# Three key tiles in a burst of value matmuls instead of two, in the sequence part of an attention and Fourier kernel

## The chip, the core and the metric

The kernel runs on one core of a Trainium2 chip. The metric is device time in microseconds (us) of one execution; each kernel is run several times and the median counts. The core's engines work side by side and wait for each other by semaphores: TensorE (PE; its weight loads are shown apart as PEld), VectorE (DVE), ScalarE (ACT), GpSimd (POOL), and SyncE (SP), which here only issues DMAs. Matmul results land in PSUM, which has eight banks of 512 fp32 columns on 128 partitions. Everything else lies in SBUF.

## The reference

The result is a gate between an attention block and a two-dimensional Fourier transform of the same x (2048 rows, 640 columns, 32 heads of 20):

```python
def _A_ref(x, wqkv, wo):
    qkv = (x @ wqkv).reshape(B, S, 3, H, Dh)  # to q, k, v by head
    scores = jnp.einsum("bhqd,bhkd->bhqk", q, k) * (Dh ** -0.5)
    p = _softmax(scores, axis=-1)
    o = jnp.einsum("bhqk,bhkd->bhqd", p, v)
    return o.reshape(B, S, D) @ wo
def _B_ref(x, dft_seq_re, dft_seq_im, dft_hid_re, dft_hid_im):
    a = jnp.einsum("bsd,ed->bse", x, dft_hid_re)
    b = jnp.einsum("bsd,ed->bse", x, dft_hid_im)
    return jnp.einsum("ts,bse->bte", dft_seq_re, a) - jnp.einsum("ts,bse->bte", dft_seq_im, b)
g = _sigmoid((x * gate_w).sum(-1, keepdims=True))
return g * _A_ref(x, wqkv, wo) + (1 - g) * _B_ref(x, ...)
```

Products that need fp32 precision are made of three matmuls on rounded parts: a number is split into a rounded first part and the rest (`split`, L110), and `part1*part1 + part1*rest + rest*part1` is summed.

## The kernel before

After an opening stage (projections to q, k, v, up to about 250 us), the kernel is one long stream of attention work with other matmuls poured into its gaps.

**Attention.** 32 units follow each other; a unit is a pair of heads and half of the queries. A unit has 32 *steps*; a step is one key tile of 128 keys by 512 queries, for both heads. For each step PE does two score matmuls, called `e`: one for each head, keys by queries (L907). ACT takes their exponent out of PSUM into an SBUF tile `p` (L909). The softmax needs the largest score of each query beforehand. For that PE computes the scores a second time, queries by keys, 41 steps ahead; these two score matmuls a step are called `m` (L187), and DVE reduces each of them to its row maxima (L189). When a unit's maxima are complete, they are reduced once more (L203), transposed on PE (L221), split (L114, L115) and sent by four small DMAs into spare rows of the query stack (L229, L230). The two heads sit in partitions 0 to 63 and 64 to 127, so a score matmul uses one half of PE's rows and two of them can run side by side.

**Value matmuls.** Two steps make one key tile for all 1024 queries of the unit. For each key tile PE does four matmuls of the exponents with the values (L528), for two heads and two query blocks, each in its own quarter of PE's columns. They add up in one PSUM bank, `av`, over the 16 key tiles of a unit. At a unit's end ACT copies `av` out (L536). These are fp32 matmuls, and the trace shows each as two records.

**Cycles and fills.** The stream is cut into cycles of four steps. A cycle is written out as a string: `e`, `m`, `F` (a fill) and `B`. `B` is the burst, the value matmuls of two key tiles in a row. An `F` is one or two fill units. A fill unit is two matmuls of 320 columns, one in each half of the rows, into the banks `yp0` and `yp1`. There are three parts of the stream by what the fills are: the hidden transform (56 cycles, L363), the sequence transform (168 cycles, L608, from about 608 to 1668 us), and the output projection (32 cycles, L715).

**PSUM.** Scores take turns in five banks, `ps0` to `ps4` (`bank`): a score matmul must wait until ACT or DVE has read the score five places earlier. `av`, `yp0` and `yp1` are the other three banks.

**The sequence part.** It consists of seven products of eight *blocks* each (56 blocks). A block is one output tile of 128 rows: 16 sequence tiles, three fill units each, so 48 fill units in three cycles. For the stationary side, a chunk of 1024 columns of the transform matrix, eight sequence tiles, is loaded by SP into a `raw` tile. POOL then adds a second matrix to it where the product asks for it (L501, products 0, 2, 3, 5 and 6 counted from 0) and splits it into a `part` tile (L114, L115). A block takes two chunks. There are three `part` buffers; each chunk's split is put on POOL's queue in the middle of the chunk two before it. For the moving side, 16 tiles `x` of the next product are made during the present one from its second block on: loaded into `araw`, added where asked for (L517), split (L114, L115). This is a *preparation*; `run_extras` does at most one in a burst. At a block's end ACT and DVE sum the two banks (L627, L628), and POOL adds the result to earlier partial results (`finish_y`, L742). POOL also does the final multiplication of each attention unit (L560).

POOL executes its queue strictly in the order written, as each engine does.

## Time and profile before

| | us |
|---|---|
| runs of before | 1867.67, 1870.73, 1872.45 (median 1870.73) |
| the profiled execution | 1869.47 |
| its span, first to last instruction | 1867.7 |
| PE, DVE, ACT, POOL busy | 1858.3, 1383.7, 1272.1, 1162.6 |

The profile has instructions with their start, duration and the event that ended the idle time before them. Records of PE matmuls overlap, so "busy" says that something was in flight, not that PE ran at its peak. The granted clock is 0.98 in the first 100 us, 0.97 in the last stretch, and 1.00 in every 100 us between; so durations can be compared across the stream.

### The profile page before, as it was taken

To read this page: it belongs to the slowest core of one execution; us is meant where nothing else is said; L and a number is where in the kernel's file an instruction comes from. 1 tells how busy PE (TensorE), PEld (TensorE's weight loads), DVE (VectorE), ACT (ScalarE), POOL (GpSimd) and SP (SyncE) were. 2 spreads that over 40 slices of the span, in tenths; PEclk is the share of its full clock that TensorE was granted. 3 is DMA by queue.
4 is the path that set the end of the run, shared out by engine and by line. 5 is a ranking of instruction groups with operands and counts; after the bars stand their busy time and mean duration, and the time that the engine had idled before them with its cause. 6 is when DMAs were issued, how large, how long until landed. Compare 5 with 4: busy or idle time off the path is not lost.

```text
span 1867.7 us, 45004 instructions
## 1 busy us (share of the span) xinstructions
PE 1858.3 (100%) x17606; PEld 1360.8 (73%) x17606; DVE 1383.7 (74%) x2310; ACT 1272.1 (68%) x2439; POOL 1162.6 (62%) x1038
## 2 busy tenths in 40 slices
PE   9999999999999999999999999999999999999998
PEld 8988777676767777777777777767777777776666
DVE  3044458787878888888888888888888888888853
ACT  4222258787877777777777777777777777778885
POOL 3335432121146897466799899867779989635544
PEclk9999999999999999999999999999999999999999
DMA  6744341222134674535567576546476766431233
GB/s 230 174 136 151 139 127 56 78 65 68 54 99 139 209 209 142 161 128 175 185 192 241 163 249 191 176 140 179 145 240 203 214 198 202 142 90 47 88 98 108
DMA packets 178771, 281.61 MB, mean 151 GB/s; under 512 B 44811, under 2 KB 113547, under 8 KB 178559
## 3 DMA queue, kind: packets, MB, share of 16 engines
q1 hardware_dynamic: 177599, 276.77, 47.4%
q0 software_dynamic: 960, 1.97, 0.6%
q8 instruction: 138, 2.26, 0.5%
q14 instruction: 74, 0.61, 0.1%
HBM read 214.61 MB, written 63.52 MB: 149 GB/s over the span
## 4 chain that ended last, share of the span: by engine, by line
PE 98%; DMA 1%; POOL 0%; ACT 0%; DVE 0%; issue 0%; SPq 0%; POOLq 0%; ACTq 0%
PE av L528 25%; PE yp L608 19%; PE ps L907 16%; PE ps L187 15%; PE yp L363 7%; PE ps L118 4%; PE ps L120 4%; PE ps L119 4%; PE yp L715 3%; PE ps L221 0%; DMA p<-in_xa 0%; POOL p L115 0%; DMA a_scr<-raw 0%; DVE mx L189 0%; ACT p L323 0%
## 5 line engine op out<-in xcount | busy, mean ns | idle before, releaser
L189 DVE TENSOR_REDUCE mx<-ps 128x1 f32<-128x512 f32 x2048 | 1280.1, 684 | 298.9 <-PE ps L187 280.7
L909 ACT ACTIVATE p<-ps 128x512 f32<-128x512 f32 x2048 | 1109.1, 599 | 371.6 <-PE ps L187 248.9
L187 PE MATMUL ps<-kst,qst 60*128 60x512 f32 x1920 | 758.3, 410 | 0.0
L907 PE MATMUL ps<-qst,kst 62*128 62x512 f32 x1920 | 744.9, 407 | 0.1
L608 PE MATMUL yp<-x,part 64*128 64x320 f32 x5376 | 662.1, 306 | 0.3 <-ACT raw L373 0.3
L608 PEld LDWEIGHTS yp<-x,part 64*128 64x128 f32 x5376 | 624.7, 186 | 8.3 <-ACT raw L373 0.6
L528 PE MATMUL av<-p,v 128*21 128x512 f32 x4096 | 490.1, 596 | 0.0
L907 PEld LDWEIGHTS ps<-qst,kst 62*128 62x128 f32 x1920 | 348.1, 185 | 182.5 <-DVE mx L189 132.2
L187 PEld LDWEIGHTS ps<-kst,qst 60*128 60x128 f32 x1920 | 342.2, 184 | 7.9 <-issue 4.2
L115 POOL TENSOR_TENSOR part<-raw,part 128x1024 fp32r<-128x1024 f32 (+1 forms) x128 | 288.0, 2250 | 10.3
L528 PEld LDWEIGHTS av<-p,v 128*21 128x21 f32 x4096 | 97.6, 100 | 221.5 <-issue 218.3
L363 PE MATMUL yp<-wb,x 64*128 64x320 f32 x1920 | 224.0, 307 | 0.0
L374 POOL TENSOR_TENSOR raw<-raw 128x320 f32<-128x320 f32 x64 | 55.7, 870 | 268.4 <-ACT raw L373 219.1
L363 PEld LDWEIGHTS yp<-wb,x 64*128 64x128 f32 x1920 | 210.1, 186 | 6.0
L114 POOL CAST part<-raw 128x1024 fp32r<-128x1024 f32 (+1 forms) x128 | 126.1, 985 | 127.9 <-PE ps L187 67.0
L501 POOL TENSOR_TENSOR raw<-raw,raw 128x1024 f32<-128x1024 f32 x77 | 185.9, 2414 | 7.5 <-DMA raw<-in_cdft 6.0
L115 POOL TENSOR_TENSOR x<-araw,x 128x320 fp32r<-128x320 f32 x112 | 97.8, 873 | 9.0
L715 PE MATMUL yp<-x,part 64*128 64x320 f32 x768 | 102.2, 308 | 0.0
L323 ACT ACTIVATE p<-ps 128x512 f32<-128x512 f32 x40 | 23.8, 597 | 102.0 <-PE ps L120 85.5
L715 PEld LDWEIGHTS yp<-x,part 64*128 64x128 f32 x768 | 92.0, 186 | 1.0
L118 PE MATMUL ps<-x,part 128*128 128x512 f32 x200 | 80.7, 403 | 1.6 <-ACT x L112 1.3
L114 POOL CAST p<-p 128x512 fp32r<-128x512 f32 x40 | 24.7, 618 | 92.4 <-ACT p L323 92.4
(110 smaller groups left out, 1419.5 us busy)
## 6 DMA issues: line engine op xcount, KB each, us to landing
raw<-in_cdft SPq DMA_DIRECT2D x192, 512.0 KB
araw<-a_scr SPq DMA_DIRECT2D x192, 160.0 KB
qk_scr<-p SPq DMA_DIRECT2D x40, 512.0 KB
kst<-qk_scr SPq DMA_DIRECT2D x84, 160.0 KB
qst<-qk_scr SPq DMA_DIRECT2D x84, 160.0 KB
yt<-y_scr SPq DMA_DIRECT2D x80, 160.0 KB
a_scr<-raw SPq DMA_DIRECT2D x64, 160.0 KB
y_scr<-yt SPq DMA_DIRECT2D x64, 160.0 KB
```

The costliest lines, as they stand in the source:

```text
L114: e1.tensor_copy(dst1, src)
L115: e2.tensor_tensor(dst2, src, f32(dst1), op=ALU.subtract)
L118: pe.matmul(ps, st1, mv1, start=first, stop=False)
L187: pe.matmul(ps, q[b : b + KROWS, qt * P : (qt + 1) * P], k[b : b + KROWS, kc * 512 : (kc + 1) * 512], start=True, stop=True)
L189: return lambda: dve.tensor_reduce(mx[n][:, h, qt, kc : kc + 1], ps, axis=AX.X, op=ALU.max)
L363: pe.matmul(yp[h][:, :HE], x[r, xz, d, cs], w[r, wz, d, :HE], start=d == 0 and z == 0, stop=d == ND - 1 and z == 2)
L501: pool.tensor_tensor(raws[0], raws[0], raws[1], op=ALU.add if PRODUCTS[n][0][1][0] > 0 else ALU.subtract)
L528: pe.matmul(av[32 * j : 32 * j + DH + 1, :], v[:, kt, h * (DH + 1) : (h + 1) * (DH + 1)], pp[qc][:, h, :], start=kt == 0, stop=kt == NS - 1)
L608: pe.matmul(yp[h][:, :HE], c[r, cz, cs], a[r, az], start=s == 0 and z == 0, stop=s == NS - 1 and z == 2)
L715: pe.matmul(yp[h][:, :HE], o[oz][r], wos[d, hf][r, wz], start=d == 0 and z == 0, stop=end)
L907: pe.matmul(pt, k[b : b + KROWS + 2, kt * P : (kt + 1) * P], q[b : b + KROWS + 2, qc * 512 : (qc + 1) * 512], start=True, stop=True)
L909: act.activation(pts[n, kt, qc][:, h], pt, AF.Exp, scale=float(DH) ** -0.5)
```

## The change

A cycle of the sequence part now has six steps: twelve `e`, twelve `m`, 24 fill units, and a burst of three key tiles. A block has two such cycles. The other parts keep four steps and two key tiles. The strings and the places of the fills:

```diff
 ORDERS = (
     ("ememFFFeFFmeFFmFeFmFeFmFmFFeFemB", (0, 0, 1, 0), (1, 1, 0, 1)),
+    ("ememeFFFFmeFFemFeFmFemFeFeFmeFFmeFFFFmmemmB", (0, 0, 0, 1, 0, 1), (1, 1, 0, 1, 0, 0)),
+    ("emFeFmFeFFmFeFFmeFFmeFFmFmFeFmeB", (1, 0, 1, 1), (0, 1, 0, 0)),
     ("emFFeFmFeFFmFeFmFeFFmeFmFFmFemeB", (0, 1, 1, 0), (1, 0, 0, 1)),
-    ("emFeFmFeFFmFeFFmeFFmeFFmFmFeFmeB", (1, 0, 1, 1), (0, 1, 0, 0)),
 )
...
 for u in range(UNITS):
-    edge.append(edge[-1] + 3)
+    edge.append(edge[-1] + 2)
...
 def burst(c):
     for n in ends:
         max_nm(n)
-    run_extras(max(done - HIDS, 0) // 3, 2)
-    for kt in (2 * c, 2 * c + 1):
-        av_step(now[0], kt // NS, kt % NS)
+    k, _, i = phase(c)
+    steps = 6 if k == 1 else 4
+    run_extras(steps - 2)
+    run_preps()
+    for kt in range(i // 2, (i + steps) // 2):
+        av_step(now[0], kt // NS, kt % NS, kt % NS == 0 and kt > i // 2)
...
             else:
                 score(kind)
+            if k == 1 and x == len(order) // 2:
+                run_preps()
```

`run_preps` is the second half of the old `run_extras`; in the sequence part it is called in the middle of a cycle too, so four times a block, where it was three times.

Since 16 key tiles don't divide by three, a burst can hold the end of one unit and the start of the next. The `av` bank is then not a fixed one: six banks are in the ring, one of them is `av`, and a unit that starts inside a burst takes the bank that was used longest ago and gives the old one back. A new `av` has 32 columns of each head's values written (not 21), so that all of its 128 partitions are defined. The value tile gets 16 more columns, which POOL clears.

```diff
-    def bank():
-        return ps_w.tile([P, 512], F32, name=f"ps{next(turn) % 5}")
+    places = collections.deque(f"ps{k}" for k in range(6))
...
+    def next_av():
+        places.append(av["name"])
+        av["name"] = places.popleft()
+        av["tile"] = place_tile(av["name"])
```

Seven steps' exponents are alive at a burst, so `p` has seven buffers (it had five). The room comes from `part`: four buffers of 4 KB a partition, not three of 8 KB. A chunk is split in two halves of 512 columns (four sequence tiles), each into a buffer of its own, the first in the middle of the chunk two before it, the second at the start of the chunk before it. The addition is done once, ahead of the first half.

```diff
     def pair_tile():
-        return work.tile([P, 2, 512], F32, name="p", bufs=5)
+        return work.tile([P, 2, 512], F32, name="p", bufs=7)
     def part_tile():
-        return work.tile([P, 2, 1024], R, name="part", bufs=3)
+        return work.tile([P, 2, 512], R, name="part", bufs=4)
...
-        def finish():
-            c = cparts[g] = part_tile()
-            if len(raws) > 1:
+        def finish(half):
+            if not half and len(raws) > 1:
                 pool.tensor_tensor(raws[0], raws[0], raws[1], op=ALU.add if PRODUCTS[n][0][1][0] > 0 else ALU.subtract)
-            split(c[:, 0], c[:, 1], raws[0], pool, pool)
+            c = cparts[2 * g + half] = part_tile()
+            split(c[:, 0], c[:, 1], raws[0][:, half * 512 : (half + 1) * 512], pool, pool)
...
+        if s % 8 == 0 and g and cfin:
+            cfin.pop(0)()
         if s % 8 == 0 and g // 8 + 3 < 2 * UNITS:
-            cfin.append(load_c(g // 8 + 3))
-        if s % 8 == 4 and cfin and g // 8 + 2 < 2 * UNITS:
+            cfin.extend(load_c(g // 8 + 3))
+        if s % 8 == 4 and cfin:
             cfin.pop(0)()
...
-                extras.append((now[0] + 5, functools.partial(finish_y, out_, t, m, y)))
+                extras.append((now[0] + 3, functools.partial(finish_y, out_, t, m, y)))
```

What moves on PE, around one burst of the sequence part. Before, three scores, the burst (`av`, two key tiles of four matmuls), two scores, and then fills (`yp`):

```order
L907 MATMUL ps_18836<-qst_92,kst_90 128x512
L187 MATMUL ps_18839<-kst_89,qst_91 128x512
L907 MATMUL ps_18842<-qst_92,kst_90 128x512
L528 MATMUL av<-p,v 21x512 x8
L907 MATMUL ps_18864<-qst_92,kst_90 128x512
L187 MATMUL ps_18867<-kst_89,qst_91 128x512
L608 MATMUL yp_18870<-x_16422,part 128x320
```

In the changed kernel (L940 is the old L907, L196 the old L187, L546 the old L528, L628 the old L608), at a burst in which a unit ends after the first key tile:

```order
L196 MATMUL ps_14347<-kst_87,qst_89 128x512
L196 MATMUL ps_14350<-kst_87,qst_89 128x512
L940 MATMUL ps_14353<-qst_89,kst_87 128x512
L196 MATMUL ps_14356<-kst_87,qst_89 128x512
L196 MATMUL ps_14359<-kst_87,qst_89 128x512
L546 MATMUL ps_12559<-p,v 32x512 x4
L546 MATMUL ps_14379<-p,v 32x512 x8
L940 MATMUL ps_14390<-qst_89,kst_87 128x512
L196 MATMUL ps_14393<-kst_87,qst_89 128x512
L940 MATMUL ps_14396<-qst_89,kst_87 128x512
L196 MATMUL ps_14399<-kst_87,qst_89 128x512
L940 MATMUL ps_14406<-qst_89,kst_87 128x512
```

Five scores, four of them for maxima, now stand ahead of the burst, and five behind it before the first fill.

What moves on POOL, at the start of the preparations in product 3, where both the matrix and the `x` tiles have an addition. Before, three preparations stand among two chunks:

```order
L742 TENSOR_TENSOR yt<-yt,m 128x320 x2
L517 TENSOR_TENSOR araw<-araw 128x320
L114 CAST x_16422<-araw 128x320
L115 TENSOR_TENSOR x_16422<-araw,x_16422 128x320
L501 TENSOR_TENSOR raw<-raw,raw_16228 128x1024
L114 CAST part<-raw 128x1024
L115 TENSOR_TENSOR part<-raw,part 128x1024
L517 TENSOR_TENSOR araw<-araw 128x320
L114 CAST x_16422<-araw 128x320
L115 TENSOR_TENSOR x_16422<-araw,x_16422 128x320
L501 TENSOR_TENSOR raw<-raw,raw_16370 128x1024
```

In the changed kernel (L762 is the old L742, L532 the old L517, L515 the old L501, L115 and L116 the old L114 and L115) one preparation stands ahead of each half chunk:

```order
L762 TENSOR_TENSOR yt<-yt,m 128x320 x2
L532 TENSOR_TENSOR araw<-araw 128x320
L115 CAST x_16541<-araw 128x320
L116 TENSOR_TENSOR x_16541<-araw,x_16541 128x320
L115 CAST part<-raw 128x512
L116 TENSOR_TENSOR part<-raw,part 128x512
L532 TENSOR_TENSOR araw<-araw 128x320
L115 CAST x_16541<-araw 128x320
L116 TENSOR_TENSOR x_16541<-araw,x_16541 128x320
L515 TENSOR_TENSOR raw<-raw,raw_16411 128x1024
L115 CAST part<-raw 128x512
L116 TENSOR_TENSOR part<-raw,part 128x512
```

The 16 preparations of a product thus stand among the parts of four blocks, where they stood among those of more than five.

## The prediction

> **What bounds the kernel now.** I read the chain that ended last first (shares of the span by engine), then the sequence part as one window (length; busy us and instructions of PE, PEld, DVE, ACT, POOL; clock; DMA share), then the same window for the value matmuls alone:

> ```profile
> PE 98%; DMA 1%; POOL 0%; ACT 0%; DVE 0%; issue 0%; SPq 0%; POOLq 0%; ACTq 0%
> ```

> ```profile
> 607.80:1668.10 1060.30, 1060.30 (x10767) 762.24 (x10765) 889.52 (x1485) 766.82 (x1422) 851.63 (x682) 1.00 0.58 182
> ```

> ```profile
> 607.80:1668.10 1060.30, 321.62 (x2688) 63.90 (x2688) 1.00 0.58 182
> ```

> PE is never idle there: the end is set by PE's own stream, at full clock. The 2688 records are 168 bursts of 16. Whether "busy" is also useful is read from one cycle, in PE's timeline (start, duration, count) and, for the burst's inside, in PEld's:

> ```profile
> 1005.68 1.92 PE L528 MATMUL av<-p,v 128*21 128x512 f32 x16
> 1007.53 0.49 PE L907 MATMUL ps<-qst,kst 62*128 62x512 f32 x1
> 1007.53 0.49 PE L187 MATMUL ps<-kst,qst 60*128 60x512 f32 x1
> 1007.86 0.60 PE L608 MATMUL yp<-x,part 64*128 64x320 f32 x5
> ...
> 1011.62 0.40 PE L187 MATMUL ps<-kst,qst 60*128 60x512 f32 x1
> 1011.65 0.39 PE L907 MATMUL ps<-qst,kst 62*128 62x512 f32 x1
> 1011.97 1.92 PE L528 MATMUL av<-p,v 128*21 128x512 f32 x16
> ```

> ```profile
> 1006.13 0.12 PEld L528 LDWEIGHTS av<-p,v 128*21 128x21 f32 x4 [0.31 <-issue]
> 1006.55 0.12 PEld L528 LDWEIGHTS av<-p,v 128*21 128x21 f32 x4 [0.31 <-issue]
> ```

> A cycle lasts 6.29 us, burst to burst. From the first fill (1007.86) to the next burst (1011.97) are 4.11 us, of which the last 0.10 is the step into the burst. In the other 4.01 each half of the rows streams 7 scores of 512 columns and 16 fills of 320, 8704 columns: 0.461 ns a column, so a score takes 0.236 and a fill 0.147. All 8 scores and 16 fills of a half are 4.25 us. Four records abreast in the burst start 0.43 apart (1006.13 to 1006.55; the mean of the burst is 0.43), so four such rounds are 1.72. 6.29 - 4.25 - 1.72 leaves **0.32 us a cycle that is neither**: the scores after a burst last 0.49 instead of 0.39, the burst's last round takes longer until the next score starts, and there is the step into it.

> **What the change removes.** 168 bursts become 112 of one and a half times the work. 56 times 0.32 goes: **-17.9 us**. The new cycle would be 1.5 x (4.25 + 1.72) + 0.32 = 9.28 us. Value records, scores and fills stay as many; 32 columns of weights for 21 change only loads that lie beside matmuls (0.12 of each 0.43). The opening, the hidden part and the output part keep their order but for one cycle; I cost them at nothing, and so the 16-column clearing and the two added `p` buffers.

> **What it asks of DVE and ACT.** A score needs its bank read five scores later. DVE and ACT in that cycle (idle time before in brackets), and the sum of the two banks, once a block:

> ```profile
> 1008.09 5.07 DVE L189 TENSOR_REDUCE mx<-ps 128x1 f32<-128x512 f32 x8 [1.23 <-PE ps L187]
> ```

> ```profile
> 1008.16 3.34 ACT L909 ACTIVATE p<-ps 128x512 f32<-128x512 f32 x6
> ```

> ```profile
> 1019.62 0.49 DVE L628 TENSOR_TENSOR m<-yp,m 128x320 f32<-128x320 f32 x1 [0.17 <-ACT m L627]
> ```

> DVE reads one score in 0.63, so 12 of them take 7.6 of 9.28 us. In a burst PE gives it nothing for 6 x 0.43 + 0.32 = 2.9 us, but four of the last five scores are maxima, 2.5 us of work that lies under it. ACT's twelve take 6.7 us (0.56 each). Both fit, with little to spare: going through the new order place by place with 0.236 and 0.147, the tightest places (the `e` after one fill in the middle, and the `m` before the six fills) come when DVE is just done. The same tightness can be seen in the hidden part, whose cycle has 15 fills for 16 and also starts with four scores in a row:

> ```profile
> 445.62 1.91 PE L528 MATMUL av<-p,v 128*21 128x512 f32 x16
> 451.79 1.92 PE L528 MATMUL av<-p,v 128*21 128x512 f32 x16
> ```

> 6.17 us, where 6.29 less one fill is 6.14: 0.03 lost a cycle. I take this for the new cycle: 112 x 0.03 = **+3.4 us**, and a cycle of 9.31. The bounds are 0 and 0.2 a cycle, +22 us, if one place waits a third of a DVE reduction (0.2 of 0.63); no gain is to be had, since the sequence part now loses nothing there. DVE's sum at a block's end (0.49) stands behind the four maxima under the burst, and the transposition for a unit's maxima comes as often as now.

> **What it asks of POOL.** This is the dear part. POOL in product 3 (starts give what each really occupies), the half-size split as it occurs in the output part, and POOL's load by product (length, busy us; products 1, 2, 3, 5):

> ```profile
> 1103.92 1.29 POOL L560 TENSOR_TENSOR o<-o,rb 128x512 f32<-128x512 f32 x1
> 1105.17 2.41 POOL L501 TENSOR_TENSOR raw<-raw,raw 128x1024 f32<-128x1024 f32 x1
> ...
> 1111.12 0.88 POOL L517 TENSOR_TENSOR araw<-araw 128x320 f32<-128x320 f32 x1
> 1112.06 0.45 POOL L114 CAST x<-araw 128x320 fp32r<-128x320 f32 x1
> 1112.59 0.87 POOL L115 TENSOR_TENSOR x<-araw,x 128x320 fp32r<-128x320 f32 x1
> 1113.42 2.41 POOL L501 TENSOR_TENSOR raw<-raw,raw 128x1024 f32<-128x1024 f32 x1
> 1115.89 1.04 POOL L114 CAST part<-raw 128x1024 fp32r<-128x1024 f32 x1
> 1117.01 2.39 POOL L115 TENSOR_TENSOR part<-raw,part 128x1024 fp32r<-128x1024 f32 x1
> 1119.37 1.70 POOL L742 TENSOR_TENSOR yt<-yt,m 128x320 f32<-128x320 f32 x2
> 1121.02 0.88 POOL L517 TENSOR_TENSOR araw<-araw 128x320 f32<-128x320 f32 x1
> ...
> 1714.77 0.61 POOL L114 CAST part<-raw 128x512 fp32r<-128x512 f32 x1
> 1715.46 1.29 POOL L115 TENSOR_TENSOR part<-raw,part 128x512 fp32r<-128x512 f32 x1
> ```

> ```profile
> 759.30:911.00 151.70, 90.54 (x77) 1.00 0.48 149
> 911.00:1062.46 151.46, 138.16 (x108) 1.00 0.63 200
> 1062.46:1214.09 151.63, 138.78 (x114) 1.00 0.66 206
> ...
> 1365.49:1517.08 151.59, 139.46 (x109) 1.00 0.66 203
> ```

> A preparation is 2.30 (1111.12 to 1113.42), an addition 2.47, a chunk's split 3.48 (1115.89 to 1119.37), two `finish_y` 1.65, the final multiplication 1.25. A half split is 0.69 + 1.26 = 1.95 (the next one starts 0.03 before a subtraction's recorded end), so a chunk costs 3.90 for 3.48: **0.42 more, 112 times**. Alone that is free where POOL has room (60% busy in product 1). Products 2, 3 and 5 are 91 to 92% busy over their whole length, and more during the preparations, which now come two a cycle. One cycle uses one chunk: 2 x 2.30 + 2.47 + 3.90 = 10.97 us of POOL against 9.31 of PE. POOL falls behind by 1.66 a cycle, plus its other work.

> How much of that can it bear? In product 1 a chunk's split waits for PE to give back its buffer, and starts at once when the last fill on it has ended (cast and its wait; PE's last fill of that chunk):

> ```profile
> 839.37 1.04 POOL L114 CAST part<-raw 128x1024 fp32r<-128x1024 f32 x1 [3.67 <-PE ps L187]
> ```

> ```profile
> 838.99 0.45 PE L608 MATMUL yp<-x,part 64*128 64x320 f32 x3
> ```

> So I start from a POOL that waits for buffers. In the new order a cycle's first 12 fill units end about 3.6 us into it (13 scores and 12 fills by the prices above, and the 0.3 that a fill takes to land), and its first fill stands at 0.8. In cycle X the first half is given back at 3.6 and split at 5.55. Then come, in product 3, two `finish_y` (1.65), a preparation, a half, a preparation, an addition and a half (2.30 + 1.95 + 2.30 + 2.47 + 1.95): 18.2. That half is needed at 3 x 9.31 + 0.8 = 28.7, a margin of 10.5. The remaining seven prepared cycles cost POOL 7 x 10.97 + 3 x 1.65 + 1.25 = 83.0 and PE 65.2: the margin ends at -7.3, and PE waits that long in all. In products 2 and 5 (one `finish_y` a block): margin 11.3, then 80.5 against 65.2, **-4.0** each. In product 0 (none): 12.1, 78.0 against 65.2, -0.7. In products 1 and 4 the chunks have no addition, and there is room. Together 7.3 + 4.0 + 4.0 + 0.7 = **+16.0 us**. After the preparations POOL needs about 7 of 9.31 a cycle and catches up before the next product's. The bounds are 0 and 25: a microsecond of margin counts about 3.5 times, and I trust the margin to 2.5 us. Before, the same account gives 2 x 5.95 + 3 x 2.30 + 1.65 = 20.5 against 18.9 a block, under 1.6 behind for 5.3 blocks, which the margin covers; and indeed no wait for POOL shows on PE.

> [...]

> **The sum.** -17.9 + 3.4 + 16.0 = +1.5 us on the profiled execution's 1869.47 (span 1867.7 and 1.8 around it): 1871.0. That execution is 1.3 under the median of the three runs, 1870.73, so against the median it is 1872.3. I say **1872**: no change that shows. The two large terms are of one cause each and of opposite signs.

> **Rivals.**
> - *POOL's lag doesn't reach PE.* It needs 7.3 us more margin than I count in product 3. For it: POOL's spans are rough, and no wait of this kind is in the trace. Against: the casts' and subtractions' starts repeat to 0.1 us, and the load is a plain sum. Time: 1872.3 - 16.0 = 1856, 0.8% faster.
> - *The banks become the bound.* Four maxima at the end of a cycle and five scores before the first fill leave DVE always just in time; from a wait of 0.1 us a cycle on, the loss counts. At 0.2 a cycle: +22.4. The cycle is then 9.48, which gives POOL's margin 0.17 x 10 = 1.7 more in each product: 16.0 falls to about 10. -17.9 + 22.4 + 10 = +15, so 1885, slower. For it: DVE's 1.23 of idle time a cycle lies wholly in the burst now, and the burst grows by 0.86. Against: DVE's share of the cycle doesn't rise by more than 0.32 in 18.9. [...]
> - *The bursts' transition isn't saved whole*, because a change of bank inside a burst (two of three units) costs as much as a cycle's: 14 of the 21 unit ends there, 0.1 to 0.3 each, under 5 us. It shifts the sum within the forecast's own range.

> **How the numbers follow.** Forecast, within 5.6 us of 1870.73 (0.3%, about what a measurement here can tell from no change): 0.40. POOL's lag at most half of what I count, the first rival and the way to it: 0.34. Banks, or POOL worse than counted: 0.26. So faster 0.34, same 0.40, slower 0.26. The range goes from the first rival's 1856 to the second's 1885; its ends leave out a tenth on each side. The forecast's own range is 1865 to 1877.

> **What would show it.** In the changed profile: bursts of 24 records, 112 of them, 9.28 to 9.31 us apart in products 1 and 4 (6.29 and 0.32 right); longer cycles only in the later preparations of products 3, 2 and 5, with PE's or PEld's fills waiting for POOL's `part` subtraction, 7, 4 and 4 us in all; POOL without idle time there. Cycles of 9.4 or more everywhere, with scores waiting for DVE, would be the second rival; none longer than 9.31, the first. Late maxima rows (the four small DMAs now have four steps of time in one unit of three) would show as `e` scores that wait for a DMA; I expect none.

## The result, and the profile after

The changed kernel takes **1900.12 us** (median of four runs, 1899.02 to 1903.87) against 1869.40 for the kernel before on the same chip (four runs, 1867.67 to 1872.45). The ratio is 1.0166, with a 95% interval of 1.0145 to 1.0187: 31 us slower. The prediction said 1872 and, at the most, 1885. The profiled execution took 1903.9 us (span 1902.1).

The same three views as before, for the changed kernel: the chain that ended last, the sequence part as one window, and in it the value matmuls.

```profile
PE 87%; DMA 6%; POOL 5%; issue 1%; DVE 0%; ACT 0%; SPq 0%; POOLq 0%; DVEq 0%; ACTq 0%
```

```profile
609.66:1699.90 1090.24, 1071.71 (x10749) 776.57 (x10747) 885.26 (x1481) 715.88 (x1418) 884.15 (x914) 0.99 0.59 176
```

```profile
609.66:1699.90 1090.24, 315.05 (x2688) 76.53 (x2688) 0.99 0.59 176
```

The chain is PE for 87% of the span, where it was 98%; 11% are now transfers and POOL. PE is idle for 18.5 of the 1090 us (1090.24 less 1071.71), where it was never idle, and its mean clock is 0.99, not 1.00. The sequence part is 30 us longer. So the loss is waiting, and something with the clock.

Where PE waits, its own timeline says (start, duration, count; in brackets the wait and what ended it). Of nine waits over 0.3 us in the sequence part, these are five:

```profile
993.87 0.49 PE L196 MATMUL ps<-kst,qst 60*128 60x512 f32 x1 [2.92 <-DVE mx L198]
...
1167.08 0.41 PE L628 MATMUL yp<-x,part 64*128 64x320 f32 x2 [1.60 <-POOL part L115]
1168.44 0.56 PE L628 MATMUL yp<-x,part 64*128 64x320 f32 x4 [0.33 <-POOL part L116]
...
1203.96 0.79 PE L196 MATMUL ps<-kst,qst 60*128 60x512 f32 x1 [3.76 <-DVE mx L198]
...
1519.49 0.79 PE L196 MATMUL ps<-kst,qst 60*128 60x512 f32 x1 [5.72 <-DVE mx L198]
```

The other four are 1.65 and 0.88 for DVE, 0.77 and 0.33 for POOL. In all PE waits 14.9 us for DVE and 3.0 for POOL's parts. The wait that I predicted is there and smaller than forecast; the large one is another.

**What DVE waits for.** The longest case, in the timeline of the changed kernel: ACT's copy of a unit's output, what SP issues after it, DVE, and PE.

```profile
1489.05 0.60 ACT L554 ACTIVATE o<-ps 128x512 f32<-128x512 f32 x1 [1.49 <-PE ps L546]
...
1500.66 0.55 SPq L562 DMA_DIRECT2D l_scr<-o  x1
1501.26 0.96 SPq L881 DMA_DIRECT2D qst<-qk_scr  x2
1503.06 0.35 SPq L768 DMA_DIRECT2D y_scr<-yt  x1
1504.17 2.75 SPq L510 DMA_DIRECT2D raw<-in_cdft  x2
1506.96 1.03 SPq L881 DMA_DIRECT2D qst<-qk_scr  x2
1508.04 0.34 SPq L565 DMA_DIRECT2D lc<-l_scr  x1
...
1511.37 1.29 DVE L198 TENSOR_REDUCE mx<-ps 128x1 f32<-128x512 f32 x2 [0.18 <-PE ps L196]
1518.64 0.25 DVE L568 RECIPROCAL lc<-lc 128x16 f32<-128x16 f32 x1 [5.99 <-DMA lc<-l_scr]
...
1513.13 0.64 PE L628 MATMUL yp<-x,part 64*128 64x320 f32 x4
```

At a unit's end its softmax sums (one row for each head and query block in `o`) go out by a DMA (`store_l`, L562) and come back spread over 128 partitions (`load_l`, L565). DVE takes their reciprocal (L568). The reciprocal stands at a fixed place of DVE's queue, 16 steps behind the unit's end, and the maxima written behind it start only after it (the next at 1518.81). Here the sums were stored 11.0 us after `o` was complete (1489.65) and their load was issued 18.4 us after it. DVE is done with the maxima ahead of the reciprocal at 1512.66, and stands for 5.99 us. All maxima behind it wait; PE's scores find no free bank and PE stops at 1513.8. The same steps in the kernel before, for the same unit:

```profile
1462.17 0.60 ACT L536 ACTIVATE o<-av 128x512 f32<-128x512 f32 x1 [0.98 <-PE av L528]
...
1476.39 0.33 SPq L547 DMA_DIRECT2D lc<-l_scr  x1
...
1485.79 0.24 DVE L550 RECIPROCAL lc<-lc 128x16 f32<-128x16 f32 x1
```

There the load was issued 13.6 us after `o` and the reciprocal found it landed, at 23.0. Over all units of the sequence part the load came at the latest 15.4 us after `o` before the change; after it, six came between 19.0 and 22.9. SP's waits (total us, times, longest) show why SP, which issues nearly all DMAs (1456 of the 1468 in the trace), one after the other as they are written, is late. First before, then after:

```profile
SPq L512 <- POOL araw L517: 32.3, 15, 4.3
...
SPq L495 <- POOL raw L501: 31.4, 16, 5.9
```

```profile
SPq L527 <- POOL araw L532: 68.1, 30, 7.7
SPq L510 <- POOL raw L515: 63.9, 26, 5.8
```

SP waits twice as long until POOL gives up a raw tile (`araw` of a preparation, `raw` of a chunk). So POOL's lateness can reach PE by a detour: POOL, SP's queue, the sums, DVE's queue, the banks. But it is not the only source. SP's longest waits between a unit's `o` and the load of its sums, in the changed kernel, first for the case above, in product 5 (window 1490 to 1508.2), then for the unit behind the first stall, in product 0 (661.5 to 682):

```profile
SPq L510 <- POOL raw L515: 5.5, 2, 4.2
SPq L510 <- POOL part L116: 2.2, 1, 2.2
```

```profile
SPq L881 <- DMA qst<-qk_scr: 2.5, 2, 1.4
SPq L527 <- DMA raw<-in_cdft: 1.8, 1, 1.8
```

In products 3, 5 and 6 most of this waiting is for POOL. In product 0, and likewise in product 2, 11 to 12 us of it ended with earlier transfers of SP's own and less than 1 with POOL. SP has 23 and 25 transfers to issue there between `o` and the load of the sums, where the kernel before has 11. Both sources make the sums late in the same way.

**What the clock does.** Four windows around that stall (window; length, then busy us and counts of PE, PEld, DVE, ACT and POOL; granted clock, DMA share, GB/s):

```profile
1500.00:1513.40 13.40, 13.40 (x144) 10.87 (x141) 10.55 (x17) 10.05 (x21) 13.03 (x12) 1.00 0.86 232
1513.40:1517.40 4.00, 0.38 (x5) 0.11 (x1) 0.00 (x0) 0.91 (x2) 3.84 (x5) 0.99 1.03 201
1517.40:1524.20 6.80, 4.71 (x27) 3.15 (x31) 3.93 (x8) 1.52 (x3) 6.53 (x7) 0.50 0.73 250
1524.20:1530.00 5.80, 5.80 (x60) 3.93 (x54) 3.96 (x8) 3.09 (x7) 2.15 (x2) 1.00 0.10 34
```

After the stall the granted clock is 0.50 for 6.8 us. The trace has six such stretches in the sequence part, of 3.4 or 6.8 us, 27.3 us together; the kernel before has none there. In 2.8 us of them PE still stood. At clock 0.50 PE works at half the rate: in a burst that falls into such a stretch (1207.57) the rounds of four value records start 0.85 us apart, for 0.43 at full clock. So the other 24.5 us cost some 12 us (an estimate, 24.5 / 2).

Where the 30.7 us of the sequence part (56 blocks, by the starts of the bursts) come from is best read from the lengths of the cycles, each against a cycle of its kind without a stall. The cycles with a wait for the sums, and those at half clock behind them, are together about 25 us too long; those in which fills wait for POOL's parts about 10 us, half clock included (PE's idle time shows only a part of these, since scores can run while the fills stand: no fill starts between 1167.57 and 1168.44, and only 0.33 us of that counts as idle, as a score runs from 1167.72). All other cycles together are about 4 us better than before, not the 14.5 us that I forecast for the part without POOL. What became of that is seen in bursts of product 1, with a transposition (L230) in the last cycle:

```profile
766.29 2.79 PE L546 MATMUL ps<-p,v 128*32 128x512 f32 x24
775.62 2.78 PE L546 MATMUL ps<-p,v 128*32 128x512 f32 x24
785.04 2.78 PE L546 MATMUL ps<-p,v 128*32 128x512 f32 x24
794.36 2.78 PE L546 MATMUL ps<-p,v 128*32 128x512 f32 x24
797.08 0.28 PE L230 MATMUL ps<-ident,nm 128*16 128x128 f32 x1
804.23 2.78 PE L546 MATMUL ps<-p,v 128*32 128x512 f32 x24
```

A plain cycle lasts 9.32 to 9.33 us, which is close to the 9.31 of the forecast. The one with a reciprocal in its middle (775.62) lasts 9.42, the one with the transposition 9.87 (9.82 in the median). In the kernel before a transposition cost 0.2 us (6.49 for 6.29), and a cycle with a reciprocal was no longer than a plain one.

### The profile page after: what moved, and what is told of

The parts are those of the page before. It is cut to its first block, busy times and chain, and to the rows that moved or that the text cites. A ratio compares the mean times of both kernels' runs of the same rounds, so it can differ in the third digit from the quotient of the medians.

```text
span 1902.1 us, 45057 instructions
## 1 busy us (share of the span) xinstructions
PE 1873.0 (98%) x17606; PEld 1378.5 (72%) x17606; DVE 1379.9 (73%) x2309; ACT 1223.6 (64%) x2439; POOL 1197.9 (63%) x1281
## 4 chain that ended last, share of the span: by engine, by line
PE 87%; DMA 6%; POOL 5%; issue 1%; DVE 0%; ACT 0%; SPq 0%; POOLq 0%; DVEq 0%; ACTq 0%
PE ps L546 22%; PE yp L628 15%; PE ps L940 15%; PE ps L196 13%; PE yp L378 7%; PE ps L119 4%; PE ps L120 4%; PE ps L121 4%; PE yp L735 3%; DMA lc<-l_scr 2%; DMA raw<-in_wo 1%; DMA raw<-in_cdft 1%; POOL raw L515 1%; POOL x L116 1%; DMA araw<-a_scr 1%; POOL part L116 1%
## 5 line engine op out<-in xcount | busy, mean ns | idle before, releaser
L942 ACT ACTIVATE p<-ps 128x512 f32<-128x512 f32 x2048 | 1059.6, 610 | 444.4 <-PE ps L196 319.4
L940 PE MATMUL ps<-qst,kst 62*128 62x512 f32 x1920 | 734.8, 409 | 0.4
L196 PE MATMUL ps<-kst,qst 60*128 60x512 f32 x1920 | 672.1, 414 | 14.0 <-DVE mx L198 14.0
L628 PE MATMUL yp<-x,part 64*128 64x320 f32 x5376 | 635.9, 309 | 3.2 <-POOL part L115 2.4
L628 PEld LDWEIGHTS yp<-x,part 64*128 64x128 f32 x5376 | 603.9, 187 | 10.8 <-POOL part L115 3.1
L546 PE MATMUL ps<-p,v 128*32 128x512 f32 x4096 | 484.4, 601 | 0.0
L940 PEld LDWEIGHTS ps<-qst,kst 62*128 62x128 f32 x1920 | 342.9, 186 | 149.1 <-DVE mx L198 85.5
L196 PEld LDWEIGHTS ps<-kst,qst 60*128 60x128 f32 x1920 | 321.2, 186 | 27.7 <-DVE mx L198 15.9
L116 POOL TENSOR_TENSOR part<-raw,part 128x512 fp32r<-128x512 f32 x240 | 308.5, 1286 | 19.2
L546 PEld LDWEIGHTS ps<-p,v 128*32 128x32 f32 x4096 | 113.6, 110 | 246.6 <-issue 241.7
L115 POOL CAST part<-raw 128x512 fp32r<-128x512 f32 x240 | 146.7, 611 | 149.2 <-PE ps L940 114.4
L515 POOL TENSOR_TENSOR raw<-raw,raw 128x1024 f32<-128x1024 f32 x77 | 183.8, 2386 | 4.1 <-DMA araw<-a_scr 2.1
L116 POOL TENSOR_TENSOR x<-araw,x 128x320 fp32r<-128x320 f32 x112 | 97.8, 873 | 9.0
L735 PE MATMUL yp<-x,part 64*128 64x320 f32 x768 | 102.7, 309 | 0.0
L735 PEld LDWEIGHTS yp<-x,part 64*128 64x128 f32 x768 | 91.9, 186 | 1.1
L338 ACT ACTIVATE p<-ps 128x512 f32<-128x512 f32 x40 | 23.7, 597 | 103.1 <-PE ps L121 100.0
L119 PE MATMUL ps<-x,part 128*128 128x512 f32 x200 | 80.5, 403 | 3.2 <-ACT x L113 3.0
L115 POOL CAST p<-p 128x512 fp32r<-128x512 f32 x40 | 25.2, 629 | 92.8 <-ACT p L338 92.8
```

Of the source, the lines that this page charges most:

```text
L115: e1.tensor_copy(dst1, src)
L116: e2.tensor_tensor(dst2, src, f32(dst1), op=ALU.subtract)
L119: pe.matmul(ps, st1, mv1, start=first, stop=False)
L196: pe.matmul(ps, q[b : b + KROWS, qt * P : (qt + 1) * P], k[b : b + KROWS, kc * 512 : (kc + 1) * 512], start=True, stop=True)
L515: pool.tensor_tensor(raws[0], raws[0], raws[1], op=ALU.add if PRODUCTS[n][0][1][0] > 0 else ALU.subtract)
L546: pe.matmul(t[32 * j : 32 * j + 32, :], v[:, c0 + h * (DH + 1) : c0 + h * (DH + 1) + 32], pp[qc][:, h, :], start=kt == 0, stop=kt == NS - 1)
```

## Experiments

In the expectations, theory A is the chain just told: GpSimd and SP late, the sums late, the reciprocal at the head of VectorE's queue, TensorE stopped, its clock halved. The other letters are explained where they stand. All kernels derive from the changed one unless it is said otherwise. In the table the ratio is to runs of the kernel before on the same chip in the same rounds. The last seven columns are the mean length of a block in each product, worked out from the starts of the bursts in the traces; "half clock" is the time at clock 0.50 within the sequence part.

| run | median us | ratio to before (95%) | half clock us | 0 | 1 | 2 | 3 | 4 | 5 | 6 |
|---|---|---|---|---|---|---|---|---|---|---|
| before | 1869.40 | | 0 | 19.04 | 18.96 | 18.93 | 18.96 | 18.92 | 18.95 | 18.92 |
| changed | 1900.12 | 1.0166 (1.0145, 1.0187) | 27.3 | 19.26 | 18.88 | 19.48 | 20.52 | 18.88 | 20.47 | 19.03 |
| no additions | 1876.29 | 1.0037 (1.0023, 1.0052) | 10.2 | 19.68 | 18.90 | 19.14 | 18.90 | 18.91 | 18.87 | 19.37 |
| three rounds | 1878.08 | 1.0047 (1.0031, 1.0064) | 6.8 | 18.79 | 18.89 | 18.87 | 19.82 | 18.88 | 18.99 | 19.40 |
| reciprocal at 22 | 1884.98 | 1.0090 (1.0075, 1.0105) | 6.8 | 18.76 | 18.88 | 19.15 | 20.24 | 18.88 | 19.57 | 18.89 |
| reciprocal at 24 | 1885.47 | 1.0086 (1.0069, 1.0103) | 6.8 | 18.73 | 18.85 | 19.14 | 20.20 | 18.82 | 19.69 | 18.90 |
| raw loads later | 1883.92 | 1.0076 (1.0061, 1.0092) | 3.4 | 18.93 | 18.88 | 19.14 | 19.98 | 18.87 | 19.35 | 18.87 |
| before, with halves | 1874.85 | 1.0032 (1.0021, 1.0044) | 0 | 19.03 | 18.92 | 18.95 | 19.43 | 18.94 | 19.16 | 19.01 |
| three rounds, reciprocal at 24 | 1870.13 | 1.0004 (0.9994, 1.0013) | 0 | 18.72 | 18.84 | 18.84 | 19.21 | 18.85 | 18.85 | 18.88 |
| the same, first fill earlier, rows earlier | 1865.64 | 0.9981 (0.9972, 0.9989) | 3.4 | 18.68 | 18.79 | 18.80 | 19.25 | 18.78 | 18.86 | 18.78 |

**The sums' two DMAs from ACT's queue.**

```diff
-            sp.dma_start(l_scr[n], o.rearrange("(j r) c -> j r c", j=4)[:, DH])
+            act.dma_start(l_scr[n], o.rearrange("(j r) c -> j r c", j=4)[:, DH])
...
-            sp.dma_start(lc, l_scr[n].rearrange("j (a b) -> (j a) b", b=16))
+            act.dma_start(lc, l_scr[n].rearrange("j (a b) -> (j a) b", b=16))
```

> The changed kernel with the two DMAs of the sums (store and load back) issued by ACT instead of SP; nothing else moves. If the place in SP's queue makes them late (theory A): they go out 1 to 10 us after the unit's end, no reciprocal waits, about 1875 us, plus a little for ACT's issuing. Rival C (the DMA engines are too full, since the loads of the preparations come closer together): the load still lands late and the reciprocal still waits, 1890 us or more.

It took 1927.69 us, ratio 1.0313 (1.0296 to 1.0330): worse still. ACT's timeline:

```profile
1153.93 0.51 ACTq L562 DMA_DIRECT2D l_scr<-o  x1
1154.49 1.09 ACT L942 ACTIVATE p<-ps 128x512 f32<-128x512 f32 x2 [16.48 <-DMA yt<-y_scr]
```

The store stands at the head of ACT's queue until it can be issued, and the exponents behind it wait for 16.5 us. By the profile that wait ended with a transfer of SP's (`yt<-y_scr`), so the store was still behind SP's lateness; it only changed its engine. This leaves open what the run was meant to tell apart; it shows that a DMA whose condition is late must not stand in the queue of an engine that PE waits for.

**No additions.** POOL's additions of two chunks (L515; 80, of which 77 lie in the sequence part's window) are left out; the transform then uses one matrix only.

```diff
-            if not half and len(raws) > 1:
+            if False:
```

> The changed kernel without POOL's addition of the second transform matrix (77 additions of 2.39 us left out, so the output is not the reference's); all DMAs stay. Theory A (POOL's lag is the root): POOL is never behind, no wait for parts and none at the reciprocal, full clock: the sequence part takes 56 blocks of 18.87 us, about 1868 us. Rival C (DMA traffic is the root): hardly better than 1900, 1890 or more. Rival D (the new order of scores itself costs more than I see in products 1 and 4): between, 1875 to 1885.

1876.29 us, 8 above theory A. Products 3 and 5 are clean (18.90 and 18.87 a block), and with 2.47 us a cycle less to do POOL delays no part: that half holds. The time lies in rival D's range, but not for its reason, since the clean products cost no more than before. DVE still waits for sums, in products 0, 2 and 6, three times:

```profile
DVE lc L568 <- DMA lc<-l_scr: 7.8, 3, 3.8
```

These loads were issued 22 to 23 us after `o`. Before the first two, SP's waits again ended with its own earlier transfers (12 to 14 us, with POOL less than 0.5), before the third mostly with POOL (6.6 us). So POOL's additions alone don't make SP late. Rival C's time is far off, but the waits of products 0 and 2 are of its kind.

**Three rounds of preparations for two cycles**, where the changed kernel has four (the kernel before had three for the same work):

```diff
-            if k == 1 and x == len(order) // 2:
+            if k == 1 and x == len(order) // 2 and (c - HID) % 2:
```

> The changed kernel with three preparations a block as before the change (the call in the middle of a cycle only in every second cycle). Theory A: POOL's lag at the end of the preparations is about 5 us less in each full product; the waits for parts go (3 us and two stretches of half clock), the reciprocal waits shrink: 1872 to 1885 us. If the packing of the preparations is the whole cause: 1868. If it is not a cause: 1900.

1878.08 us, within theory A's range: 22 of the 31 us are back. Products 0, 2 and 5 are almost clean; waits for sums of 4.1 and 3.1 us remain in products 3 and 6. The second round in every cycle gives POOL and SP more in the same time, and most of the loss hangs on it; which of the two counts for how much, this run doesn't tell.

**The reciprocal later.**

```diff
-        steps = (6, 10, 16, 23, 27, 34, 45) if n < NU - 4 else (1, 4, 7, 8, 11, 14, 16)
+        steps = (6, 10, 22, 27, 31, 38, 45) if n < NU - 4 else (1, 4, 7, 8, 11, 14, 16)
```

> The changed kernel with one line of numbers altered: a unit's reciprocal of the sums is put 22 steps behind the unit's end, not 16 (some 9.4 us later, still in a cycle's middle), and the store and load of its result 4 steps later each; nothing is left out. Theory A (the reciprocal stands at the head of VectorE's queue while SP's late load of the sums is on its way; TensorE stops behind it and then gets half its clock): the five waits of 1.1 to 6.0 us before the reciprocal are gone, and the half-clock stretches behind them too; left are some 3 us of waits for GpSimd's parts and one or two stretches of 3.4 us: about 1875 us (1870 to 1880). Rival B (TensorE is held by GpSimd falling behind, the reciprocal only shows it): the stalls come back at another place, as waits for parts, and the time stays at 1890 to 1900.

1884.98 us. (The edit also moves the store and the loads behind the reciprocal 4 steps, and POOL's multiplication.) No reciprocal waits any more, though loads are still issued up to 23.1 us after `o`. So the waits at the reciprocal cost 15 us, net. But 10 us more remain than theory A's middle, 5 more than its range. The chain of waits, and one wait of PE, with this edit:

```profile
PE 88%; POOL 7%; DMA 3%; issue 1%; SPq 0%; DVE 0%; ACT 0%; POOLq 0%; ACTq 0%
```

```profile
1139.56 0.42 PE L628 MATMUL yp<-x,part 64*128 64x320 f32 x2 [1.59 <-POOL part L115]
```

DMA falls from 6 to 3% of the chain, POOL rises from 5 to 7%. Products 2, 3 and 5 are 0.27, 1.36 and 0.69 a block above product 1, times eight 18.6 us; this is POOL's part now, for about 10 in the changed kernel. The reading that fits: each stall had given POOL time to catch up, and without the stalls its lag reaches PE itself. Rival B, which expected 1890 or more, was right in kind and too large.

The same with 24 steps (`(6, 10, 24, 29, 32, 39, 45)`), where the reciprocal falls into the last step of a cycle:

> The changed kernel with the reciprocal 24 steps behind the unit's end: that is the last step of a cycle, where VectorE is idle before the burst, not its middle; nothing is left out. Theory A: as with 22 steps, and the 0.1 us that a plain cycle with a reciprocal in its middle takes longer (9.42 for 9.32) goes as well, for some 28 units 3 us: about 1872 us (1866 to 1877), 2 to 4 us below the run with 22 steps. Rival B: 1890 to 1900, as with 22 steps. If the 0.1 us comes from something else than the reciprocal's place, the two runs are equal.

1885.47 us, no different in the median, and again above theory A's range. In products 1 and 4 the block falls from 18.88 to 18.85 and 18.82, as the 0.1 us per reciprocal would have it (3 units in 8 blocks, 0.04 a block); that is 2 us in 56 blocks, too little beside runs that scatter by 4.

**Raw loads half a chunk later.** In the changed kernel a chunk's raw tile is read half a chunk longer, by the second half's split, but its next load is issued as early as before.

```diff
-        if s % 8 == 0 and g // 8 + 3 < 2 * UNITS:
-            cfin.extend(load_c(g // 8 + 3))
         if s % 8 == 4 and cfin:
             cfin.pop(0)()
+        if s % 8 == 4 and g // 8 + 3 < 2 * UNITS:
+            cfin.extend(load_c(g // 8 + 3))
```

> The changed kernel with one edit: SP issues a chunk's loads into the raw tiles in the middle of the chunk three ahead of it, half a chunk later than now, so that a raw tile has again as long between its last read and its next load as in the kernel before; the reciprocal stays in its place, nothing is left out. Theory A (SP is late because its in-order queue stands before loads whose raw tile GpSimd still holds for a second half; that makes the sums' loads late): SP's waits for GpSimd before these loads fall from 64 to some 30 us, the sums' loads are issued within 17 us of a unit's end as before, most waits before the reciprocal go, and the time comes to about 1885 us (1878 to 1890), as with the reciprocal put later. Rival E (SP is late through the four rounds of preparations and the stack loads, the raw tiles matter little): loads of the sums still up to 21 us behind a unit's end, stalls of several us, 1893 to 1902 us.

1883.92 us, in theory A's range. SP's wait for the raw tiles falls from 63.9 us to

```profile
SPq L510 <- POOL raw L515: 27.7, 12, 4.2
```

and only two reciprocals still wait (0.7 and 1.6 us). The latest loads are still at 20 and 22 us, not within 17 as theory A had it; these are the units of products 0 and 2, where SP waits for its own transfers, and the two reciprocals are theirs. This edit, one in the order of a single queue, is worth as much as moving the reciprocal out of the way: the two mend the same thing from two ends. What is left is again mostly POOL.

**The kernel before with half parts.** The granules of 4 KB alone (two halves, four buffers), in the old cycle of two key tiles:

```diff
-        return work.tile([P, 2, 1024], R, name="part", bufs=3)
+        return work.tile([P, 2, 512], R, name="part", bufs=4)
...
-            cfin.append(load_c(g // 8 + 3))
+            cfin.extend(load_c(g // 8 + 3))
```

> The kernel before with one part of the change alone: the parts are made and kept in granules of 4 KB (two halves of a chunk, four buffers), in the old cycle with two key tiles to a burst; nothing is left out. Theory A (halving costs GpSimd some 0.2 us for each extra instruction, and holds the raw chunk's buffer half a chunk longer; the old cycle has room for both, since its reciprocal had 7.6 us of margin): within 0.3% of before, 1866 to 1874 us, with no wait of TensorE over 1 us and no half-clock stretch. Rival D (the granules are what falls behind, whatever the cycle): the stalls of the products with two input chunks (P3, P5) and the half clock appear here too, 1880 us or more.

1874.85 us, ratio 1.0032 (1.0021 to 1.0044), just beyond what theory A allowed. It is the same fault in a light form: loads of sums up to 20.8 us after `o` (15.4 before), and three reciprocals that wait:

```profile
DVE lc L552 <- DMA lc<-l_scr: 7.4, 3, 3.4
```

So the smaller granules, with their longer hold on the raw tiles, cost about 6 us in the old cycle; if they cost as much in the new one, that is 6 of the 31.

**Three rounds and the reciprocal at 24 together.**

> The changed kernel with two edits: the second round of preparations, in a cycle's middle, only in every second cycle (three rounds for two cycles, where each cycle has two), and the reciprocal 24 steps behind the unit's end; nothing is left out. Theory A: the run with three rounds of preparations alone took 1878 us, with stalls of 4.1, 3.1, 0.5 and 0.5 us before reciprocals and one stretch of 6.8 us at half clock; those 8.2 + 3.4 us go, and 0.1 us for each of some 28 reciprocals: about 1864 us (1861 to 1869), below the kernel before. Rival B (the rounds of preparations set the lateness, the reciprocal's place nothing): 1876 to 1880, as without the second edit.

1870.13 us, ratio 1.0004 (0.9994 to 1.0013): no difference from the kernel before. That is 1 us above theory A's range and 6 below rival B's. No reciprocal waits, no half clock is left, and 3 us remain in product 3 (POOL). With nearly all losses mended, the longer burst has gained next to nothing. With raw loads later as a third edit it became worse:

> The changed kernel with three edits: three rounds of preparations for two cycles, the reciprocal 24 steps behind a unit's end, and the raw loads half a chunk later; nothing is left out. Without the third edit the time was 1870 us, with the reciprocal off the path and 3 us lost in product 3. Theory A: the third edit has little left to free, since no reciprocal waits: 1866 to 1871 us. Rival F (the raw loads half a chunk later come too late for GpSimd's addition): product 3 and 5 grow, 1875 us or more.

1874.91 us, ratio 1.0028 (1.0019 to 1.0037); product 3 rose to 19.68 and product 2 to 19.01, while product 5 stayed at 18.86. Where the sums no longer wait, the later load only costs, nearly as much as rival F said, though not in product 5.

**Where the gain in light products goes.** The chain cycle's 0.5 us, tried at three places on top of the kernel of 1870 us. First the transposition six places later in the cycle:

```diff
-        while ends:
+        while ends and k != 1:
             max_chain(ends.pop(0))
...
+            if k == 1 and x == 6:
+                while ends:
+                    max_chain(ends.pop(0))
```

> The changed kernel with three rounds of preparations for two cycles, the reciprocal 24 steps behind a unit's end, and the transposition of a unit's maxima put not right behind the burst but six places later in the cycle, behind the five scores and the first fill; nothing is left out. Without the last edit the time was 1870 us, and a cycle with such a transposition took 9.80 us for 9.32, where it costs 0.2 us in the kernel before. Theory A (0.3 of the 0.5 us is the five scores behind the transposition, which wait for its bank and for VectorE): such a cycle takes some 9.5 us, 21 of them in the sequence part save 6 us: 1864 us (1862 to 1867). Rival G (the 0.5 us is the transposition's own, wherever it stands, or the maxima's rows come too late for the scores): 1869 us or more.

1880.17 us, ratio 1.0055 (1.0043 to 1.0068): rival G, in its second form. Cycles with a transposition took 9.95 at the least, 10.2 in the median, and in each product PE waited 0.3 to 2.7 us for the maxima rows (`qst<-m`). Then the first of the two small operations behind it on ScalarE (`split(m1, m2, pt, act, dve)`):

> The changed kernel with three rounds of preparations for two cycles, the reciprocal 24 steps behind a unit's end, and the first of the two small operations that split a unit's transposed maxima (0.28 us) done by ScalarE, not VectorE; nothing is left out. Without the last edit 1870 us, and a cycle with such a transposition took 9.80 us for 9.32. Theory H (VectorE has no room left in the new cycle, so each 0.28 us on it behind a burst comes out on TensorE): such cycles fall to about 9.55 us, 21 of them save 4 to 6 us: 1865 us (1862 to 1868). Rival G (the 0.5 us is the transposition's own on TensorE): cycles of 9.8 and 1869 to 1872 us.

1867.68 us, ratio 0.9994 (0.9985 to 1.0003). The cycles stayed at 9.80, so theory H in this form is wrong; that the time still falls into its range says nothing, since it is within the scatter of 1870. Then the first fill of the cycle two scores behind the burst:

```diff
-    ("ememeFFFFmeFFemFeFmFemFeFeFmeFFmeFFFFmmemmB", ...
+    ("emFemeFFFmeFFemFeFmFemFeFeFmeFFmeFFFFmmemmB", ...
```

> The changed kernel with three rounds of preparations for two cycles, the reciprocal 24 steps behind a unit's end, and in the string of the sequence part the first fill put behind two scores of the cycle, as in the kernel before, not behind five; nothing is left out. Without the last edit 1870 us. Theory H (the five scores in a row behind the burst wait for banks when VectorE is late by the transposition's two small operations): cycles with a transposition fall from 9.80 to some 9.6 us and plain ones stay at 9.32 or fall by up to 0.05: 1864 to 1868 us. Rival G: no change, 1869 to 1872 us; if the fill then waits for the sums of the two banks at a block's start, every second cycle grows and the time is above 1873 us.

Cycles with a transposition fall to 9.65, as theory H said, though its reason (VectorE late) is not shown (bursts in product 1 of this kernel):

```profile
788.74 2.78 PE L546 MATMUL ps<-p,v 128*32 128x512 f32 x24
791.45 0.28 PE L230 MATMUL ps<-ident,nm 128*16 128x128 f32 x1
798.38 2.78 PE L546 MATMUL ps<-p,v 128*32 128x512 f32 x24
```

and yet the time is 1875.65 us, ratio 1.0035 (1.0022 to 1.0047). SP's and PE's timelines say why:

```profile
1193.83 0.91 SPq L768 DMA_DIRECT2D y_scr<-yt  x2
1202.03 0.33 SPq L510 DMA_DIRECT2D raw<-in_cdft  x1
1202.46 0.86 SPq L620 DMA_DIRECT2D yt<-y_scr  x2
1203.41 0.67 SPq L238 DMA_DIRECT2D qst<-m  x1
...
1207.48 0.47 PE L940 MATMUL ps<-qst,kst 62*128 62x512 f32 x1 [3.00 <-DMA qst<-m]
```

The first fill issues the next raw load, which waits for POOL until 1202.0. With the fill moved ahead, this load stands in front of the maxima rows in SP's queue, where the rows stood in front of it. It is the same fault again: an urgent small transfer behind a load that waits. So the rows go one step earlier:

```diff
-            at_step(now[0] + 2, rows)
+            at_step(now[0] + 1, rows)
```

> As the run with the first fill behind two scores, with one line altered: SP issues the four small DMAs of a unit's maxima rows one step earlier, ahead of the loads that the cycle's first fill issues; nothing is left out. Theory J (these rows came too late only because SP's in-order queue had the raw load, which waits for GpSimd, ahead of them): the waits of 1.9 to 3.0 us for the rows and the half clock behind them go, cycles with a transposition stay at 9.65, and the time is 1866 us (1862 to 1869). Rival K (the rows are late because the whole chain is late: transposition, split, 10 us of landing): still 1872 us or more, with waits for these rows.

**1865.64 us, ratio 0.9981 (0.9972 to 0.9989): faster than both kernels**, by a small but measurable amount. Theory J holds: no wait for rows is left, and cycles with a transposition stay at 9.65. Its chain of waits is PE's again:

```profile
PE 98%; POOL 1%; DMA 1%; DVE 0%; issue 0%; ACT 0%; SPq 0%; POOLq 0%; ACTq 0%
```

With the small operation on ScalarE in addition:

> As the run before it, and ScalarE does the first of the two small operations on a unit's transposed maxima; nothing is left out. Theory H (VectorE has no room behind the burst): cycles with a transposition 9.6 or less, 1 to 3 us below the run before it: 1864 us (1860 to 1868). If that split is no longer on the path, both are equal.

1866.06 us, ratio 0.9980 (0.9971 to 0.9989): equal, so that split is not on the path.

## Why the prediction was wrong, point by point

- **The cycle: right.** The profile has bursts of 24 records and plain cycles of 9.32 us for 9.31. Where nothing else comes, two cycles (18.64) save 0.22 us a block on three old ones (18.86); forecast were 0.32 less 0.06.
- **"... the transposition for a unit's maxima comes as often as now": the wrong step for the light products.** It comes as often, but costs 0.5 us, not 0.2. Five scores stand behind it and no fill; moving one fill there gave half of the 0.3 back, and where the other half goes stays open. A reciprocal in mid-cycle costs 0.1 more. At three units in eight blocks that is 0.15 a block of the 0.22. The forecast for this part was -14.5 us (-17.9 + 3.4); the clean products 1 and 4 measure -0.06 a block, which is -3.5 over 56 blocks. I had asked whether DVE's work fits under a burst on average and had not gone through the one cycle in five that has more.
- **"PE waits" for POOL, +16.0: the mechanism and nearly the size are right, but hidden behind another.** The products fell behind in the order that I gave (3 and 5 most, 0, 1 and 4 not, once no reciprocal waits), and the run with the reciprocal at 22 loses 18.6 us there (half clock included) for 16.0. In the changed kernel itself only 3.0 us of PE's idle time and about 10 us by the cycles' lengths are of this kind; the larger stalls, it seems, give POOL time back.
- **The step that failed: "Late maxima rows ... I expect none" was the only small DMA that I looked at, and the account of what is behind SP stopped there.** The sum holds no term for it: "Both fit" counts DVE's work and not what DVE waits for. The change makes SP wait longer for POOL's raw tiles and puts the loads of four rounds of preparations where three stood, and the sums stand behind both in the same queue. I had the data: the load of the sums came at up to 15.4 us, the reciprocal at 23.0, so 7.6 us were left for its landing and for any delay, of which the change used up more than all. It is a wait of DVE in front of PE: 14.9 us of waits, about 25 us of cycle time with the half clock, for a term of 0. The run without these waits is 15 us faster, since POOL's part then grows from about 10 to 18.6.
- **The clock: not foreseen.** The prediction took 1.00 for granted, because the kernel before shows it there; the changed kernel's falls to 0.50 behind stalls.
- The rivals: the second, with 1885 and DVE as the engine that holds PE, came nearest, for another reason. DVE does no more work than before (885 us busy in the sequence part, 890 before); it stands still.

What stays open: why the sums' DMA took as long as 10 us from issue to landing in the case above. The windows show the DMA engines at a share of 0.86 to 1.03 there, with the next heads' stacks being loaded; the four latest loads of sums before the change, and five of the six latest after it, are those of such units. Open with it is why SP's own earlier transfers hold it up so long in products 0 and 2. No run tested either alone. The first 600 us of an execution scatter by up to 5 us among these kernels (600.1 to 605.3 from the start of the span to the last burst of the hidden part), which limits what one profiled execution tells.

## What to carry to other kernels

When a change makes one engine late, follow every queue in which something waits for it, not only the consumer: SP's queue passed the delay on to all that stood behind, and one small transfer there, the sums' load issued 18.4 us after `o`, was enough to stop PE for 5.72 us. So write down the margin of each small transfer (when issued, when needed) before the change, and put what needs its result at a place that leaves room, and no waiting load ahead of what is urgent. After that, look at the one cycle that has most to do, not at the mean.

## What the runs showed of the hardware

POOL, DVE, ACT and SP take their queues in the order written in all the cases above: what stood at the head held up the rest for 3.67 us on POOL (the split of 839.37 before the change), 5.99 on DVE (the reciprocal), 16.48 on ACT (the store of the sums) and 7.2 on SP (the raw load of the run with the first fill earlier). PE's matmuls need not start so: fills come in pairs, one for each half of the rows, and in the kernel before, in the cycle of 1005.68, five fills have started at 1008.157, a score starts at 1008.161, and the sixth fill only at 1008.398.
